# The prologue of a packed-attention and SwiGLU kernel: two moves in its written order

## The chip, the cores and the metric

The kernel runs on one core of one Trainium2 chip. The metric is the device time of the whole program in microseconds (us). The time is a median over several runs; a change of less than about 0.2% of it can't be told from none.

Engines are named as the profile names them: PE is TensorE's matrix products (PEld its loading of the stationary operand), DVE is VectorE, ACT is ScalarE, POOL is GpSimd, SP is SyncE, which here only issues DMAs.

## The reference, cut to what matters

There are 8 batches with 8 heads each, 576 positions and head size 64. A packed attention goes first: 32 packed queries `p` attend to the 576 keys and values, and then the 576 queries `q` attend to the 32 packed results, which are both keys and values there. The result, 4608 rows of 512, goes through a SwiGLU layer of width 1536 whose weights come as 64-bit numbers.

```python
def sm_attn(qq, kk, vv):
    s = scale * np.matmul(qq, kk.transpose(0, 1, 3, 2))
    s = s - np.max(s, axis=-1, keepdims=True)
    a = np.exp(s)
    a = a / (np.sum(a, axis=-1, keepdims=True) + 1e-09)
    return np.matmul(a, vv)
p_packed = sm_attn(p, k, v)
out = sm_attn(q, p_packed, p_packed)
...
g = x @ w_gate
silu = g * (1.0 / (1.0 + np.exp(-g)))
val = x @ w_val
return (silu * val @ w_out).astype(np.float32)
```

## The kernel before, in words

**Folding.** The attention's output is a weighted mean over 32 packed rows per head. So the kernel multiplies the packed rows with the gate and value weights first (`m_mm`, one matrix `mh` per batch and pair of weight chunks), and then multiplies the second attention's weights `a2` with that. Steps are named by the attention they belong to: `s1_` for the first one (scores, maximum, exponential, turning, packing, scaling), `s2_` for the second.

**Weights.** The 64-bit numbers arrive in twelve chunks of 1 MB (`load_w`, tile `st`) and are turned into fp32 by five instructions on 128x1024 elements (`f64_convert`): two on ACT (lines 124 and 125) and three on DVE, which are a clamp (line 126), a shift with an or (line 127), and an or with an and (line 128). `step("W", k)` issues the next one of the five for chunk k. A chunk's fp32 form is complete after line 128; only then may `m_mm` read it.

**Prologue.** Batch 0 has nothing to hide behind. Its stages stand in an order written by hand, within a block where PE, DVE, ACT and SP all keep the program's order; each engine runs its instructions strictly in that order, and waits where an operand isn't there. The order around the change is: load everything; the first attention's scores, exponentials, turned copies and packing (`s1_pack`, into one PSUM bank); four steps of weight chunk 0; `s1_scale` (line 288, packed result times reciprocal sum, tile `pp`); the fifth step; `s1_flip` (line 298, `pp` turned on PE) and `s1_ppt` (line 302, copied by ACT to `ppt`); the second scores of the first half of the queries, `s2_mm(0, 0)`, read by two 32x32 block transposes on DVE, `s2_block(0, 0)` (line 438); the folded weights of chunk 0, `m_mm` and `m_high` (line 524, ACT copies to `mh`); `s2_max` (lines 452 and 453) and `s2_exp` (line 457); and the second half's `s2_mm(0, 1)` and `s2_block(0, 1)`.

**Padding.** `warm_up(n)` puts n products of the identity with itself into PE's queue, with no input from any other engine. Eighteen of them stand between the scores and the first products of the SwiGLU layer, and 25 more behind those (the word `warm25` in the program's text). The profile counts two matmul records for each fp32 product.

**After the padding.** `back(0)` (line 716) turns the first half's attention weights into `a2f`. The first products of the SwiGLU layer, `gv(0)` (line 742), read `a2f` and `mh`. From there PROGRAM lists the order for the rest of batch 0 word by word (`W2` is a step of chunk 2, `g0` is `gv(0)`, `M:1.0` a folded product). Batches 1 to 7 follow in a loop with a plan by chunk.

**Banks.** PSUM has three rings here: `acc` (4 banks), `gv` (2) and `aux` (2). In the prologue `ps()` hands out `acc` and `gv` banks in turn. The scores, folded products and packing all draw on these, and `gv(0)` takes the two `gv` banks next.

Of the kernel before, what the change touches and what calls it, by code (L numbers as in the profile page):

```python
# [59 lines left out]
def tile_pack_attention_swiglu(ctx: ExitStack, tc: tile.TileContext, qT, kT, v, vq, pT, wgv, wout, out):  # L60
# [30 lines left out]
    def pin(ins):  # L91

        return tc.keep_in_program_order(ins) if steady[0] else ins

    def ps():
        turn[0] += 1
        if wide[0] and turn[0] % 2:
            return ps_acc.tile([P, 512], F32, tag="acc", name="acc_aux")
        if wide[0]:
            return ps_gv.tile([P, 512], F32, tag="gv", name="gv_aux")  # L100
        return ps_aux.tile([P, 512], F32, tag="aux", name="aux")
# [33 lines left out]
    def convert_w(fc):  # L135
        return f64_convert(w_t[fc // 2][:, :, fc % 2, :], sts.pop(fc), NHP)
# [12 lines left out]
    def convert_wout(k):  # L149
        wos[k] = pair(F32, "wo_f")  # L150
        return f64_convert(wos[k], sts.pop(("out", k)), 2)
# [13 lines left out]
    def load_k(b):  # L165
        p_t = pool.tile([P, NHP, NP], F32, tag="p", bufs=2, name="p_t")
        (nc.sync if b else nc.scalar).dma_start(p_t, pT[b])
        k_t = io_tile(0, [P, 2, NHP, HS], F32, "k_t")
        if b == 0:
            qs[b] = io_tile(0, [P, 2, NHP, HS], F32, "q_t")  # L170
        for hf in range(2):
            nc.sync.dma_start(k_t[:, hf], kT[b, :, hf])
        kps[b] = (k_t, p_t)
# [16 lines left out]
    def by_head(outs, lhs, rhs):  # L190

        for hp in range(NHP):
            for par in range(NPAR):
                r = slice(64 * par, 64 * par + 64)
                nc.tensor.matmul(outs[par][32 * hp : 32 * hp + 32], lhs(r, hp), rhs(r, hp), start=True, stop=True)  # L195
# [90 lines left out]
    def s1_scale(b):  # L286
        pp = pool.tile([P, NPAR, D], F32, tag="pp", bufs=1, name="pp")
        nc.vector.tensor_tensor(
            pp,
            pps[b][0][:, : NPAR * D].rearrange("p (r d) -> p r d", r=NPAR),  # L290
            st1[b][2][:, 2].unsqueeze(2).broadcast_to([P, NPAR, D]),
            op=ALU.mult,
        )
        pps[b].append(pp)

    def s1_flip(b):
        pps[b].append(ps())
        nc.tensor.transpose(pps[b][2][:, :P], pps[b][1].rearrange("p r d -> p (r d)"), ident)

    def s1_ppt(b):  # L300
        ppts[b] = pool.tile([P, P], F32, tag="ppt", bufs=2, name="ppt")
        nc.scalar.copy(ppts[b], pps[b][2][:, :P])
# [117 lines left out]
    def s2_tiles(b):  # L420
        st2[b] = (
            pool.tile([P, 2, NPAR, HS], F32, tag="s2", bufs=1, name="s2"),
            pool.tile([P, 3, 2 * NPAR * NBK], F32, tag="r2", bufs=1, name="r2"),
        )
# [3 lines left out]
    def s2_mm(b, c, bank=ps):  # L428
        two[b, c] = [bank(), bank()]
        q_t, ppt = qs[b], ppts[b]  # L430
        by_head(
            [x[:, :HS] for x in two[b, c]], lambda r, hp: ppt[r, 32 * hp : 32 * hp + 32],
            lambda r, hp: q_t[r, c, hp],
        )

    def s2_block(b, c):
        for par in range(NPAR):
            pin(nc.vector.transpose(st2[b][0][:, c, par], two[b, c][par][:, :HS]))

    def s2_view(b, cs):  # L440
        s2, r2 = st2[b]
        n = NPAR * NBK
        rows = slice(cs.start * n, cs.stop * n)
        return (
            s2[:, cs].rearrange("p c r (k n) -> p (c r k) n", n=NP),
            [r2[:, i, rows] for i in range(3)],
            [P, (cs.stop - cs.start) * n, NP],
        )

    def s2_max(b, cs):  # L450
        x, (m, _, _), shape = s2_view(b, cs)
        pin(nc.vector.tensor_reduce(m, x, axis=AX.X, op=ALU.max))
        pin(nc.vector.tensor_tensor(x, x, m.unsqueeze(2).broadcast_to(shape), op=ALU.subtract))  # L453

    def s2_exp(b, cs):
        x = st2[b][0][:, cs].rearrange("p c r n -> p (c r n)")
        pin(nc.scalar.activation(x, x, AF.Exp, scale=SCALE))  # L457
# [10 lines left out]
    def s2_scale(b, cs):  # L468
        x, (_, _, r), shape = s2_view(b, cs)
        pin(nc.vector.tensor_tensor(x, x, r.unsqueeze(2).broadcast_to(shape), op=ALU.mult))  # L470
# [31 lines left out]
    def m_mm(b, k, fcs, plain=False):  # L502


        if (b, k) not in ms:
            dt = F32 if plain else F32R
            ms[b, k] = tuple(
                pool.tile([P, NPAR, 2, 2 * P], dt, tag=t, bufs=2, name=t) for t in ("mh", "ml")[: 1 if plain else 2]
            )
        ppt, w = ppts[b], w_t[k]  # L510
        n = (fcs.stop - fcs.start) * 2 * P
        pss = m_ps[b, k, fcs.start] = [ps(), ps()]
        by_head(
            [x[:, :n] for x in pss], lambda r, hp: ppt[r, 32 * hp : 32 * hp + 32],
            lambda r, hp: w[r, hp, fcs].rearrange("p f n -> p (f n)"),
        )

    def m_high(b, k, fcs):
        m = ms[b, k]
        n = (fcs.stop - fcs.start) * 2 * P  # L520
        for par, x in enumerate(m_ps[b, k, fcs.start]):
            at = (slice(None), par, fcs)
            src = x[:, :n].rearrange("p (f n) -> p f n", n=2 * P)
            nc.scalar.copy(m[0][at], src)  # L524
            if len(m) > 1:
                lows.append((m[1][at], src, m[0][at].bitcast(F32)))
# [114 lines left out]
    with tc.manual_schedule(engines={mybir.EngineType.PE}):  # L641
# [19 lines left out]
        with tc.manual_schedule(  # L661
# [23 lines left out]
            def step(kind, k):  # L685

                if (kind, k) not in conv:
                    conv[kind, k] = convert_w(k) if kind == "W" else convert_wout(k)
                next(conv[kind, k], None)

            for _ in range(4):
                step("W", 0)
            s1_scale(0)
            step("W", 0)
            s1_flip(0)
            s1_ppt(0)
            s2_tiles(0)
            c0, c1 = (slice(c, c + 1) for c in range(2))
            s2_mm(0, 0)
            s2_block(0, 0)  # L700
            m_mm(0, 0, c0, True)
            m_high(0, 0, c0)
            s2_max(0, c0)
            s2_exp(0, c0)
            s2_mm(0, 1)
            s2_block(0, 1)
            load_k(1)
            load_wout(0)
            warm_up(18)
# [4 lines left out]
            def back(c):  # L714
                for par in range(NPAR):
                    nc.vector.transpose(a2f[:, par, c * HS : (c + 1) * HS], st2[0][0][:, c, par])

            s2_sums(0, c0)
            s2_scale(0, c0)
            back(0)  # L720
            wide[0] = False

            rows, accs = begin(0)
# [188 lines left out]
```

## Time and profile before

| | |
|---|---|
| median of 3 runs | 749.33 us (749.03 to 750.16) |
| profiled execution | 749.33 us, its span 747.5 us |
| mean granted PE clock | 0.998 |
| busy: PE, DVE, ACT | 736.2, 455.4, 367.9 us |

Span is the time from the first to the last instruction; 1.8 us lie outside it. Busy PE doesn't mean useful PE: the padding counts too. [...] All times in the rows are us from the start of the span.

### The profile page before, as it was taken

What the parts mean: (1) busy time and instruction counts of PE and PEld (TensorE: products, weight loads), DVE (VectorE), ACT (ScalarE), POOL (GpSimd) and SP (SyncE); (2) the same over time, 40 slices, a digit from 0 to 9 for tenths busy, and PEclk for the clock granted to TensorE, in tenths of its full rate; (3) what the DMA queues carried; (4) which work ended last, traced back from release to release, by engine and by line L of the source; (5) the groups of instructions that cost most, each with busy time, mean ns of one, the idle gap of its engine ahead of it and who ended that gap; (6) DMA issues with size and microseconds to landing.
All of it is one profiled execution on the core that took longest, in us unless ns stands there. A gap on an engine that the chain in (4) does not pass through costs nothing.

```text
span 747.5 us, 15126 instructions
## 1 busy us (share of the span) xinstructions
PE 736.2 (98%) x6280; PEld 594.8 (80%) x6280; DVE 455.4 (61%) x1004; ACT 367.9 (49%) x662; POOL 2.0 (0%) x13
## 2 busy tenths in 40 slices
PE   7999999999999999999999999999999999999998
PEld 4756666888788887887888888888888888888886
DVE  5988878665756557645765556655575555744334
ACT  3777745754516445563544535464452644533331
POOL 0000000000000000000000000000000000000000
PEclk9999999999999999999999999999999999999999
DMA  9686583202112021302112022100201000010001
GB/s 354 251 313 249 182 323 114 72 3 72 64 71 69 2 72 65 124 4 72 64 57 83 3 72 64 58 3 1 72 2 71 3 1 2 1 57 1 1 1 71
DMA packets 20004, 59.15 MB, mean 79 GB/s; under 512 B 5984, under 2 KB 7008, under 8 KB 17376
## 3 DMA queue, kind: packets, MB, share of 16 engines
q1 hardware_dynamic: 19792, 58.12, 21.5%
q8 instruction: 49, 0.80, 0.5%
q14 instruction: 19, 0.16, 0.1%
q10 hardware_dynamic: 144, 0.07, 0.0%
HBM read 48.69 MB, written 9.49 MB: 78 GB/s over the span
## 4 chain that ended last, share of the span: by engine, by line
PE 90%; DVE 4%; ACT 2%; issue 1%; DVEq 0%; ACTq 0%
PE gv L558 34%; PE acc L577 29%; PE aux L195 7%; PE gv L742 6%; PE acc L768 6%; PE aux L577 4%; PE aux L410 1%; ACT L457 1%; PE gv_aux L195 1%; PE acc L646 1%; DVE hf L569 1%; PE warm_ps L646 1%; DVE hl L539 1%; DVE s L453 1%; ACT hh L105 1%
## 5 line engine op out<-in xcount | busy, mean ns | idle before, releaser
L565 ACT ACTIVATE sg<-gv 128x256 f32<-128x256 f32 (+1 forms) x168 | 68.9, 410 | 166.0 <-PE gv L558 134.7
L558 PE MATMUL gv<-a2h,ml 128*128 128x256 f32 (+1 forms) x672 | 147.2, 300 | 2.3 <-DVE t L572 1.8
L569 DVE TENSOR_TENSOR hf<-gv,sg 128x256 f32<-128x256 f32 x168 | 70.7, 421 | 121.2 <-PE gv L558 99.1
L558 PE MATMUL gv<-a2h,mh 128*128 128x256 f32 (+1 forms) x672 | 144.2, 296 | 0.0
L558 PE MATMUL gv<-a2l,mh 128*128 128x256 f32 (+1 forms) x672 | 144.0, 296 | 0.0
L577 PE MATMUL acc<-wo_h,hl 128*128 128x512 f32 x336 | 136.2, 405 | 0.0
L577 PE MATMUL acc<-wo_l,hh 128*128 128x512 f32 x336 | 132.2, 393 | 0.0
L577 PE MATMUL acc<-wo_h,hh 128*128 128x512 f32 x336 | 131.9, 393 | 0.0
L558 PEld LDWEIGHTS gv<-a2h,ml 128*128 128x128 f32 x672 | 115.1, 189 | 19.3 <-PE gv L558 4.6
L105 ACT CAST hh<-hf 128x256 fp32r<-128x256 f32 x168 | 67.9, 404 | 102.5 <-DVE hf L569 102.4
L539 DVE TENSOR_TENSOR hl<-hf,hh 128x256 fp32r<-128x256 f32 x168 | 70.5, 419 | 78.4 <-ACT hh L105 78.4
L558 PEld LDWEIGHTS gv<-a2h,mh 128*128 128x128 f32 x672 | 108.4, 189 | 0.0
L558 PEld LDWEIGHTS gv<-a2l,mh 128*128 128x128 f32 x672 | 108.1, 189 | 0.0
L577 PEld LDWEIGHTS acc<-wo_h,hl 128*128 128x128 f32 x336 | 63.2, 188 | 34.1 <-issue 26.2
L577 PEld LDWEIGHTS acc<-wo_h,hh 128*128 128x128 f32 x336 | 63.1, 188 | 14.5
L577 PEld LDWEIGHTS acc<-wo_l,hh 128*128 128x128 f32 x336 | 63.2, 188 | 7.9
L498 DVE TENSOR_TENSOR ml<-aux,mh 128x512 fp32r<-128x512 f32 x92 | 59.0, 681 | 4.7 <-ACT mh L524 3.6
L195 PE MATMUL aux<-w,ppt 64*32 64x512 f32 (+1 forms) x784 | 52.4, 588 | 0.5 <-ACT mh L524 0.5
L524 ACT CAST mh<-aux 128x512 fp32r<-128x512 f32 x92 | 49.2, 586 | 4.9 <-PE aux L195 1.9
L565 ACT ACT_TABLE_LOAD x30 | 38.5, 1283 | 16.2 <-PE gv L558 16.1
L768 PE MATMUL acc<-wo_f,h 128*128 128x512 f32 x96 | 44.2, 594 | 0.0
L768 PEld LDWEIGHTS acc<-wo_f,h 128*128 128x128 f32 x96 | 17.3, 189 | 17.2 <-issue 16.5
(149 smaller groups left out, 755.5 us busy)
## 6 DMA issues: line engine op xcount, KB each, us to landing
st<-in_wgv SPq DMA_DIRECT2D x12, 1024.0 KB, 6.4
k_t<-in_kT SPq DMA_DIRECT2D x16, 576.0 KB, 4.8
q_t<-in_qT SPq DMA_DIRECT2D x16, 576.0 KB, 4.9
out<-ot SPq DMA_DIRECT2D x36, 256.0 KB, 2.1
v_t<-in_vq SPq DMA_DIRECT2D x6, 1280.0 KB, 5.5
st<-in_wout SPq DMA_DIRECT2D x6, 1024.0 KB, 5.5
v_t<-in_v SPq DMA_DIRECT2D x2, 1024.0 KB, 8.5
p_t<-in_pT SPq DMA_DIRECT2D x7, 64.0 KB, 2.1
```

The lines of the kernel that those rows point to most:

```text
L105: e.copy(dst, src)
L195: nc.tensor.matmul(outs[par][32 * hp : 32 * hp + 32], lhs(r, hp), rhs(r, hp), start=True, stop=True)
L498: pin(nc.vector.tensor_tensor(*lows.pop(0), op=ALU.subtract))
L524: nc.scalar.copy(m[0][at], src)
L539: low = lo.tensor_tensor(hl, src, hh.bitcast(F32), op=ALU.subtract)
L558: nc.tensor.matmul(pg[:, :n], m_[:, g, f, s * P : (s + 1) * P], a_[:, g, off : off + n], start=(i == 0), stop=(i == 5),)
L565: nc.scalar.activation(sg[:, :n], pgs[0][:, :n], AF.Silu)
L569: nc.vector.tensor_tensor(hf, pgs[1][:, o : o + 256], sg[:, o : o + 256], op=ALU.mult)
L577: nc.tensor.matmul(acc[:, :], h_[:, c : c + P], w_[fc // 2][:, fc % 2], start=(fc == 0 and i == 0), stop=(fc == NFC - 1 and i == 2),)
L646: nc.tensor.matmul(at[:, :P], ident, ident, start=True, stop=True)
L742: nc.tensor.matmul(held[i][s][:, :n], m_[:, g, f, s * P : (s + 1) * P], a_[:, g, off : off + n], start=(j == 0), stop=(j == len(todo) - 1),)
L768: nc.tensor.matmul(accs[2 * is_b + c], half(i)[:, c * P : c * P + P], wos[fc // 2][:, fc % 2], start=(fc == 0), stop=(fc == NFC - 1),)
```

## The change

It changes the written order of the prologue, and no instruction. `s1_scale` now stands ahead of the fourth step of chunk 0 (line 127), instead of behind it. The fifth step (line 128) moves behind the first half's scores, their block transposes, their maximum and their exponential. The second half's scores `s2_mm(0, 1)` go ahead of the folded product `m_mm`, and their block transposes `s2_block(0, 1)` go behind `back(0)`. The padding and the loads stay where they were in the text, behind all of these but `s2_block(0, 1)`.

```diff
-            for _ in range(4):
+            for _ in range(3):
                 step("W", 0)
             s1_scale(0)
-            step("W", 0)
             s1_flip(0)
             s1_ppt(0)
+            step("W", 0)
             s2_tiles(0)
             c0, c1 = (slice(c, c + 1) for c in range(2))
             s2_mm(0, 0)
             s2_block(0, 0)
+            s2_max(0, c0)
+            s2_exp(0, c0)
+            step("W", 0)
+            s2_mm(0, 1)
             m_mm(0, 0, c0, True)
             m_high(0, 0, c0)
-            s2_max(0, c0)
-            s2_exp(0, c0)
-            s2_mm(0, 1)
-            s2_block(0, 1)
             load_k(1)
             load_wout(0)
             warm_up(18)
...
             s2_scale(0, c0)
             back(0)
+            s2_block(0, 1)
             wide[0] = False
```

On DVE, from the clamp of chunk 0 (`w_81` is that chunk, `s_229` and `s_228` are the second scores, before and after the change):

```order
 L126 TENSOR_SCALAR w_81<-w_81 128x4x256
+L288 TENSOR_TENSOR pp<-gv_aux,rs_118 128x128
 L127 SCALAR_TENSOR_TENSOR w_81<-w_81,st 128x4x256
-L288 TENSOR_TENSOR pp<-gv_aux,rs_118 128x128
+L438 STREAM_TRANSPOSE s_228<-gv_aux 128x288
+L438 STREAM_TRANSPOSE s_228<-acc_aux 128x288
+L452 TENSOR_REDUCE r_229<-s_228 128x18
+L453 TENSOR_TENSOR s_228<-s_228,r_229 128x576
 L128 SCALAR_TENSOR_TENSOR w_81<-st,w_81 128x4x256
-L438 STREAM_TRANSPOSE s_229<-gv_aux 128x288
-L438 STREAM_TRANSPOSE s_229<-acc_aux 128x288
-L452 TENSOR_REDUCE r_230<-s_229 128x18
```

The scaling goes one instruction up. The last bit operation of chunk 0 (line 128) goes from ahead of the four instructions on the first half's scores to behind them.

On PE before, the last of the eight products of the first scores, the first and last of the eight folded products, and what follows up to `gv(0)` (the banks are numbered to tell the two sets of scores apart, 231/232 and 259/260):

```order
L195 MATMUL acc_aux_232<-q_t_95,ppt_227 32x288
L195 MATMUL gv_aux_244<-w0_81,ppt_227 32x256
L195 MATMUL acc_aux_245<-w0_81,ppt_227 32x256
L195 MATMUL gv_aux_259<-q_t_95,ppt_227 32x288
L195 MATMUL acc_aux_260<-q_t_95,ppt_227 32x288
L646 MATMUL warm_ps_89<-ident_72 128x128 x18
L742 MATMUL gv_317<-a2f_298,mh_243 128x256 x2
```

And on PE after the change, the same pieces (the two sets of scores are in banks 230/231 and 246/247):

```order
L195 MATMUL acc_aux_231<-q_t_95,ppt_225 32x288
L195 MATMUL gv_aux_246<-q_t_95,ppt_225 32x288
L195 MATMUL acc_aux_247<-q_t_95,ppt_225 32x288
L195 MATMUL gv_aux_257<-w0_81,ppt_225 32x256
L195 MATMUL acc_aux_258<-w0_81,ppt_225 32x256
L646 MATMUL warm_ps_89<-ident_72 128x128 x18
L743 MATMUL gv_317<-a2f_296,mh_256 128x256 x2
```

The folded products now stand between both sets of scores and the padding; before, the second set stood there. On ACT the exponential (line 457) goes ahead of the two copies to `mh`; SP's order is the same.

## Rows read from the trace of the kernel before

**Rows 1.** Page, parts 1 and 4: busy time by engine; shares of the chain.

```profile
PE 736.2 (98%) x6280; PEld 594.8 (80%) x6280; DVE 455.4 (61%) x1004; ACT 367.9 (49%) x662; POOL 2.0 (0%) x13
PE 90%; DVE 4%; ACT 2%; issue 1%; DVEq 0%; ACTq 0%
```

**Rows 2.** Waits of PE from 24 us to the end: total, times, longest.

```profile
PE gv L558 <- DVE t L572: 1.8, 7, 0.4
PE aux L195 <- ACT mh L524: 0.5, 1, 0.5
PE gv L742 <- ACT mh L524: 0.5, 1, 0.5
```

**Rows 3.** Chain of waits, 18.1 to 36 us: start, us, what.

```profile
18.14 5.29 PE warm_ps L646 x36
23.43 1.73 PE gv L742 x8
25.16 5.58 PE acc L646 x50
30.75 0.70 PE aux L195 x16
```

**Rows 4.** Timeline of DVE: start, us, engine, line, operation, [idle before].

```profile
13.41 1.23 DVE L127 SCALAR_TENSOR_TENSOR w<-w,st 128x1024 int32<-128x1024 int32 x1
14.56 0.28 DVE L288 TENSOR_TENSOR pp<-gv_aux,rs 128x128 f32<-128x128 f32 x1
14.76 1.22 DVE L128 SCALAR_TENSOR_TENSOR w<-st,w 128x1024 int32<-128x1024 int32 x1
16.39 0.48 DVE L438 STREAM_TRANSPOSE s<-gv_aux 128x288 f32<-128x288 f32 x1 [0.41 <-PE acc_aux L195]
...
18.73 0.48 DVE L438 STREAM_TRANSPOSE s<-gv_aux 128x288 f32<-128x288 f32 x1
...
19.62 0.75 DVE L464 TENSOR_REDUCE r<-s 128x18 f32<-128x576 f32 x1
...
21.72 0.84 DVE L716 STREAM_TRANSPOSE a2f<-s 128x288 f32<-128x288 f32 x2
22.48 0.65 DVE L126 TENSOR_SCALAR w<-w 128x1024 f32<-128x1024 f32 x1
...
27.89 2.35 DVE L128 SCALAR_TENSOR_TENSOR w<-st,w 128x1024 int32<-128x1024 int32 x2
```

**Rows 5.** Timeline of PE and PEld, 11 to 18 us, same columns.

```profile
11.89 1.81 PE L271 MATMUL gv_aux<-v_t,a 128*32 128x64 f32 x80 [0.47 <-DMA v_t<-in_v]
...
15.58 0.43 PE L195 MATMUL gv_aux<-q_t,ppt 64*32 64x288 f32 x1 [0.36 <-ACT ppt L302]
...
15.90 0.40 PE L195 MATMUL acc_aux<-q_t,ppt 64*32 64x288 f32 x1
...
16.09 0.14 PEld L195 LDWEIGHTS gv_aux<-w,ppt 64*32 64x32 f32 x2 [0.33 <-issue]
...
16.41 0.38 PE L195 MATMUL acc_aux<-w,ppt 64*32 64x256 f32 x1
...
16.93 0.69 PE L195 MATMUL gv_aux<-q_t,ppt 64*32 64x288 f32 x1
```

**Rows 6.** Timeline of ACT, same columns.

```profile
15.26 0.27 ACT L302 COPY ppt<-acc_aux 128x128 f32<-128x128 f32 x1 [2.40 <-PE acc_aux L298]
...
18.91 0.68 ACT L457 ACTIVATE s<-s 128x576 f32<-128x576 f32 x1 [1.40 <-DVE s L453]
```

**Rows 7.** Stretches: length, busy us by engine, PEclk, DMA share, GB/s.

```profile
16.97:18.14 1.17, 1.17 (x17) 0.26 (x17) 1.10 (x3) 0.54 (x2) 0.00 (x0) 0.50 1.02 413
18.14:20.36 2.22, 2.22 (x11) 2.22 (x11) 2.17 (x4) 1.45 (x2) 0.00 (x0) 0.50 0.89 273
20.36:23.43 3.07, 3.07 (x29) 3.07 (x28) 2.93 (x8) 3.07 (x5) 0.00 (x0) 1.00 1.01 398
```

**Rows 8.** Timeline of SP's DMA issues, same columns.

```profile
19.18 0.38 SPq L144 DMA_DIRECT2D st<-in_wout  x1
```

## Prediction

> **What bounds the kernel now.** I read the page's busy times first, then PE's waits, then the chain through the prologue, and last the timelines of DVE, ACT and PE around the edit. PE is busy for 98% of the span and carries 90% of the chain [rows 1]. From 24 us to the end it waits 2.8 us in all (1.8, 0.5 and 0.5) [rows 2], seven times on DVE's read of a bank and twice on ACT's emptying one, all of which PE itself has just filled. So whatever PE is late by at 24 us, it is late by at the end. The question is when PE reaches the first products of the SwiGLU layer.
>
> In the chain these start at 23.43, directly behind the 36 records of padding, which run from 18.14 for 5.29 us without a gap; behind them come 1.73 us of products, 5.58 us of the second padding, and the next folded product at 30.75 [rows 3]. The reader should see what does not stand there: DVE. It had `a2f` ready at 21.72 + 0.84 = 22.56 [rows 4], and PE took it only at 23.43. The padding is a fixed amount of work in PE's order, so the date that counts is when the padding may start, which is when the last instruction ahead of it is done.
>
> **The change part by part.** *The scaling goes ahead of line 127.* The packing ends at 11.89 + 1.81 = 13.70 [rows 5], while DVE was in line 127 from 13.41 and came to the scaling at 14.56 [rows 4]. Now DVE waits at its head and scales at about 13.75 (I add 0.05 for the hand-over), 0.81 earlier. What hangs on it goes along: flip, copy to `ppt`, scores, and the first block transpose, which came 16.39 - 14.56 = 1.83 us behind the scaling and now comes at 15.58. Line 127 starts 0.20 behind the scaling (the step from 14.56 to 14.76), at 13.95, and ends at 15.18; DVE then idles 0.40, where it idled 0.41 before [rows 4]. The new 0.44 in front of the scaling is thus lost to DVE and nothing of it is regained by shorter work.
>
> *Line 128 goes behind the maximum.* Two block transposes, the maximum and the subtraction take 18.73 - 16.39 = 2.34 us of DVE [rows 4]. So line 128 starts at 15.58 + 2.34 = 17.92 and ends at 19.14, where it ended at 14.76 + 1.22 = 15.98. That is 3.16 us later, and the folded product needs it. Before, PE went on to the folded product at 16.09, right behind the scores [rows 5]; now it can't before 19.25 (the same 0.11 behind line 128).
>
> *The second scores go ahead of the folded product.* They were 16.93 to 18.14 [rows 5, 7]; now they run right behind the first set, at about 15.3 to 16.1. Their `gv` bank is the packing's, which the scaling has emptied by 14.03. They cost PE nothing where they now are, since it waits afterwards in any case: from 16.1 to 19.25, 3.15 us. Before, PE worked through nearly all of that time.
>
> *`s2_block(0, 1)` goes behind `back(0)`.* DVE reaches the sums (line 464) at 17.92 + 1.14 = 19.06 instead of 19.62 (the exponential, at 18.91 before, moves to about 18.1 and ends by 18.8 [rows 6]). So `a2f` is ready 0.56 earlier, at 22.0, and the bank of the second scores is free at 22.4. DVE's clamp of the next chunk comes at 22.8 instead of 22.48 [rows 4]. Neither is on the path if the padding ends later than 22.4.
>
> *The clock.* PE's granted clock is 0.50 from 16.97 to 20.36 and 1.00 behind that [rows 7]. Ahead of the fall PE had next to nothing to do between the packing's end at 13.70 and the scores at 15.58 [rows 5]; in the slow stretch it worked without a pause, and then the clock rose. Rates at both levels: a set of scores took 15.58 to 15.90 + 0.40 = 16.3 at 1.00 and 1.21 at 0.50 [rows 5, 7]; the padding at 1.00 takes 5.58 / 50 = 0.112 a record [rows 3], 4.0 us for 36. Counted from its own place, 2.22 us at half rate are worth 1.11, plus 3.07 at full rate, 4.18 [rows 7]; I use 4.15. The folded product took 16.09 to 16.79 = 0.70 at full rate [rows 5], and by the ratio of the scores about 1.2 at half rate.
>
> The trace does not show how long the slow stretch gets with a gap in it. From below: it doesn't occur, the folded product ends at 19.95 and the padding at 24.1. With the clock back at 20.36 as before, the product ends at 20.4 and the padding at 24.55. From above: the whole padding runs at half rate, 8.3 us from 20.45, to 28.75. I take the stretch as ending later by the time that PE now idles in it, 20.36 + 3.15 = 23.5, because the row nearest to this case is the one where the clock rose after unbroken work. Then the padding runs 20.45 to 23.5 at half rate (worth 1.53) and 2.62 more at full rate, to 26.1.
>
> [...]
>
> *What comes behind.* `mh` is ready by about 21.2 and `a2f` with its bank by 22.4, so the end of the padding still decides. `gv(0)` starts at 26.1 instead of 23.43: 2.7 us late. The second padding and `M:1.0` follow at 33.4. The last bit operations of the next two chunks ended at 27.89 + 2.35 = 30.24 [rows 4]; DVE is some 0.3 to 0.7 us later there, ACT about 1 us (its copies to `mh` wait for the folded product, with the next chunk's two operations behind them in its order), still ahead of 33.4. These are the instructions behind the new waits, and none gets onto the path. On SP, `load_k(1)` waits for the second scores to leave `q_t` and can only go earlier; the load of the output weights behind it was issued at 19.18 [rows 8] and needs the tile that line 128 leaves at 19.14, so it goes at about the same time; I price the DMAs at nothing.
>
> The sum: -0 (earlier scores, hidden by the wait), + 2.7 (the padding starts at 20.45 instead of 18.14, which is 3.16 for the folded product's later start, less 0.85 for what stands between its start and the padding's, 1.2 now and 18.14 - 16.09 = 2.05 before; and it takes 5.65 instead of 5.29), - 0 to 1 (the two waits on ACT later [rows 2], which I keep, since they are for copies of PE's own products). The profiled execution took 749.33, which is also the median of the runs: 749.33 + 2.7 = 752.0.
>
> **The rivals.**
>
> *A shorter slow stretch.* The clock rises where it did, or never falls: padding ends at 24.55 or 24.1, +1.1 or +0.7, 750.4 or 750.0. For it: the gap falls into the slow stretch itself, where idling is free. Against: the work that ended the stretch is what the change takes out.
>
> *The padding at half rate all through.* +5.3, 754.6. For it: nothing on record has shown a rise after a gap of 3 us. Against: in the trace unbroken work brought the clock up well within the padding's length.
>
> *Given back later.* PE's waits behind 24 us are 2.8 in all [rows 2]; if DVE and ACT, which don't get later by as much, used the time to be ahead, most of the loss is returned and the time is 749.3 to 749.8. Against: the waits are on results of PE's own products some hundred ns before.
>
> *Faster: the first SwiGLU products wait for `a2f` and not for the padding.* Then the earlier sums decide: `gv(0)` at 22.4 instead of 23.43, -1.0, 748.3. It decides only if the padding is over by 22.4, so started by 18.25 and the folded product by 17.55 at full rate. That needs line 128 to end 1.7 us before the 19.14 worked out. For it: all of DVE's dates up to `a2f` do move ahead. Against: DVE starts line 128 no earlier than 17.92.
>
> **How the numbers follow.** Forecast (752.0, own range 751.0 to 753.2): 0.68. Shorter slow stretch: 0.16. All at half rate: 0.05. Given back: 0.07. Faster: 0.04. The range 750.0 to 753.4 leaves out the returned and the faster case and the half-rate one, 0.16, and takes in the shorter stretch. The bound of 0.2% is 1.5 us, so no change reaches from 747.8 to 750.8. Slower: 0.68 + 0.05 and a fifth of the shorter stretch, 0.76. Same: the rest of that and the returned case, 0.20. Faster: 0.04.
>
> **What would show it.** Right: in PE's timeline a gap of about 3 us behind two sets of scores, ended by DVE's line 128; the folded products at about 19.2; granted clock 0.50 beyond 20.4; padding without a gap directly ahead of `gv(0)` at 25 to 27; DVE's `a2f` ready near 22, some 4 us unused; and the same length from `gv(0)` to the end. Wrong: `gv(0)` released by DVE; folded products before 18; or PE's distance from `gv(0)` to the end shorter by over 1 us.

## The result and the profile after

The changed kernel takes 752.86 us (median of 5, 752.46 to 754.38) against 749.33 us (748.65 to 750.36) before; the ratio is 1.0044, with a 95% interval of 1.0031 to 1.0058. That is 3.5 us slower, inside the range and on the side that was forecast, and 0.9 above the forecast of 752.0. The profiled execution is the median one, with a span of 751.1 us.

The timeline of DVE after the change (start, length, engine, line, operation, idle time before it) answers to [rows 4]:

```profile
14.29 0.29 DVE L288 TENSOR_TENSOR pp<-gv_aux,rs 128x128 f32<-128x128 f32 x1 [0.91 <-PE gv_aux L271]
14.50 1.22 DVE L127 SCALAR_TENSOR_TENSOR w<-w,st 128x1024 int32<-128x1024 int32 x1
16.13 0.48 DVE L438 STREAM_TRANSPOSE s<-gv_aux 128x288 f32<-128x288 f32 x1 [0.42 <-PE acc_aux L195]
...
18.47 1.22 DVE L128 SCALAR_TENSOR_TENSOR w<-st,w 128x1024 int32<-128x1024 int32 x1
19.61 0.75 DVE L464 TENSOR_REDUCE r<-s 128x18 f32<-128x576 f32 x1
...
21.70 0.84 DVE L716 STREAM_TRANSPOSE a2f<-s 128x288 f32<-128x288 f32 x2
22.46 0.44 DVE L438 STREAM_TRANSPOSE s<-gv_aux 128x288 f32<-128x288 f32 x1
```

DVE waits for the packing at the head of its queue (0.91), idles 0.42 again until the scores, and finishes line 128 at 19.69, where it was 15.98. The attention weights `a2f` are there at 22.54, as before. PE's timeline after, answering to [rows 5]: the last product of the second scores, the first of the folded products, and both paddings around `gv(0)`.

```profile
16.12 0.40 PE L195 MATMUL acc_aux<-q_t,ppt 64*32 64x288 f32 x1
19.84 0.60 PE L195 MATMUL gv_aux<-w,ppt 64*32 64x256 f32 x1 [3.31 <-DVE w L128]
...
20.88 6.06 PE L646 MATMUL warm_ps<-ident 128*128 128x128 f32 x36
26.77 1.89 PE L743 MATMUL gv<-a2f,mh 128*128 128x256 f32 x8
28.50 5.74 PE L646 MATMUL acc<-ident 128*128 128x128 f32 x50
```

PE stands still for 3.31 us, released by line 128. The chain of waits after (start, length, what) answers to [rows 3]:

```profile
18.56 1.15 DVE w L128
...
20.95 5.99 PE warm_ps L646 x36
26.93 1.73 PE gv L743 x8
28.66 5.58 PE acc L646 x50
34.24 0.70 PE aux L195 x16
```

Line 128 is now in the chain, and behind it every piece keeps its length but the padding, 5.99 instead of 5.29. `gv(0)` starts at 26.93 instead of 23.43, 3.50 later; from there to the end of the span it is 751.1 - 26.93 = 724.2 us, and before it was 747.5 - 23.43 = 724.1. Nothing was given back. The stretches (length, busy us of PE, PEld, DVE, ACT and POOL, granted clock of PE, DMA share, GB/s), answering to [rows 7]:

```profile
17.00:18.00 1.00, 0.00 (x0) 0.00 (x0) 0.96 (x2) 0.00 (x0) 0.00 (x0) 0.90 0.97 393
18.00:19.00 1.00, 0.00 (x0) 0.00 (x0) 1.00 (x2) 0.35 (x1) 0.00 (x0) 0.50 0.91 376
...
20.95:24.31 3.36, 3.36 (x16) 3.36 (x17) 3.33 (x7) 3.29 (x5) 0.00 (x0) 0.50 1.04 413
24.31:26.93 2.62, 2.62 (x23) 2.62 (x23) 2.58 (x4) 2.62 (x4) 0.00 (x0) 0.94 0.23 88
```

The clock reads 1.00 up to 17.75 and falls at about 17.8. It reads 0.50 up to 24.60 and 1.00 from 24.80, and so rises at about 24.6 (0.94 over 2.62 us is 0.31 us at 0.50 and the rest at 1.00). It is at 0.50 for 6.8 us instead of the 3.4 of [rows 7]. Half and full rate stand here for a clock of 0.50 and of 1.00: at 0.50, from 20.95 to 24.31, 16 records of padding took 3.36 us, 0.21 each, against 5.58 / 50 = 0.112 at 1.00 [rows 3].

### The profile page after: what moved, and what is told of

Same layout as the page of the kernel before. It is cut to its first block, busy times and chain, and to the rows that moved or that the text cites. A ratio compares the mean times of both kernels' runs of the same rounds, so it can differ in the third digit from the quotient of the medians.

```text
span 751.1 us, 15127 instructions
## 1 busy us (share of the span) xinstructions
PE 737.4 (98%) x6280; PEld 595.8 (79%) x6280; DVE 456.1 (61%) x1004; ACT 368.6 (49%) x662; POOL 2.0 (0%) x13
## 4 chain that ended last, share of the span: by engine, by line
PE 92%; DVE 4%; ACT 2%; issue 1%; POOL 0%; DVEq 0%; ACTq 0%; POOLq 0%
PE gv L558 34%; PE acc L577 29%; PE aux L195 7%; PE gv L743 6%; PE acc L769 6%; PE aux L577 4%; PE aux L410 1%; PE warm_ps L646 1%; ACT L457 1%; PE gv_aux L195 1%; PE acc L646 1%; DVE s L453 1%; DVE hf L569 1%; DVE hl L539 1%; DVE r L452 1%
```

## The experiments

Two theories stood against each other. The first is the prediction's: line 128's date holds the folded product, PE idles, and both the late start and the longer stretch at the half rate push the padding and all that follows. The rivals put the loss on other moves of the change, or deny the clock a part in it. Each ratio below is to the kernel before as timed beside that run. Its median there was 749.58 us for the four kernels with line 128 early, line 128 late, 8 and 10, and 7 and 18, and 749.16 us for the other four; small differences between two kernels are therefore taken from the ratios.

**Line 128 early again, the rest as changed.**

```diff
             s1_ppt(0)
             step("W", 0)
+            step("W", 0)
             s2_tiles(0)
...
             s2_exp(0, c0)
-            step("W", 0)
             s2_mm(0, 1)
```

> The change with one part of it undone: chunk 0's last bit operation (line 128) again directly behind line 127, the rest as changed. Theory: line 128's date is what holds the folded product, so that product starts at about 17.0 instead of 19.84, PE hardly idles in front of it, and the padding ends near 23.3; the clock's slow stretch is then about as in the kernel before. gv(0) near 23.5, total 749.3 (748.6 to 750.0). Rival: the loss comes from the other moves (the second scores ahead, their transposes behind the first half's turning, the scaling); then the time stays near 752.9.

Measured: 749.15 us, ratio to before 0.9995 (0.9986 to 1.0003). The whole loss is gone; the other moves cost nothing that can be measured. PE's timeline of this kernel, the first of the folded products, the first padding and `gv(0)`:

```profile
17.14 0.40 PE L195 MATMUL gv_aux<-w,ppt 64*32 64x256 f32 x1 [0.90 <-DVE s L438]
...
17.73 4.29 PE L646 MATMUL warm_ps<-ident 128*128 128x128 f32 x36
22.55 1.97 PE L743 MATMUL gv<-a2f,mh 128*128 128x256 f32 x8 [0.54 <-ACT st L125]
```

The folded product came at 17.14, as expected, but what it waited for last was a bank that DVE still read (line 438); line 128 was done by then. The padding ran at full rate (the granted clock is 1.00 throughout in this execution) and ended at 22.0, so `gv(0)` came not at 23.5, as expected, but at 22.55. The wait is put down to an instruction of ACT on a weight chunk, which `gv(0)` doesn't read; I take only the date from it. DVE's timeline names the likelier one:

```profile
21.93 0.84 DVE L716 STREAM_TRANSPOSE a2f<-s 128x288 f32<-128x288 f32 x2
22.69 0.44 DVE L438 STREAM_TRANSPOSE s<-gv_aux 128x288 f32<-128x288 f32 x1
```

`gv(0)` starts 0.62 behind the start of the two transposes that write `a2f`, and ahead of the read of the second scores' bank at 22.69.

**Line 128 late, the rest as before.**

```diff
             s1_scale(0)
-            step("W", 0)
             s1_flip(0)
...
-            m_mm(0, 0, c0, True)
-            m_high(0, 0, c0)
             s2_max(0, c0)
             s2_exp(0, c0)
+            step("W", 0)
+            m_mm(0, 0, c0, True)
+            m_high(0, 0, c0)
             s2_mm(0, 1)
```

> The kernel before with one part of the change alone: line 128 and with it the folded product go behind the first half's maximum and exponential; scaling, second scores and their transposes stay where they were. Theory: the folded product starts at about 20.1, with PE idle from 16.3 on, and now the second scores stand between it and the padding too, so gv(0) comes at about 27.5 and the time is 753.4 (752.6 to 754.5). Rival (the other moves are the cause): 749.3 to 750.3.

Measured: 753.62 us, ratio 1.0053 (1.0041 to 1.0065). This part alone costs as much as the change. A little more was expected, since the second scores again stand between the folded product and the padding; the two intervals overlap, so that surcharge is not shown. Its waits of PE (who waited, for what: total us, times, longest):

```profile
PE gv_aux L195 <- DVE w L128: 3.8, 1, 3.8
```

**The scaling early, the rest as before.**

```diff
-            for _ in range(4):
+            for _ in range(3):
                 step("W", 0)
             s1_scale(0)
-            step("W", 0)
             s1_flip(0)
             s1_ppt(0)
+            step("W", 0)
+            step("W", 0)
```

> The kernel before with another part of the change alone: the packed result is scaled ahead of lines 127 and 128, which follow it directly; nothing else moves. Theory: the scores come earlier, but lines 127 and 128 each end later by what DVE waited for the packing (0.3 to 0.9 us, with the packing's date in that execution), so the folded product starts at 16.4 to 16.9 instead of 16.09, and padding and gv(0) stay within half a us: 749.6 (749.0 to 750.3). Rival (the earlier scaling is worth its 0.8 us): 748.8. Rival (it is the scaling that costs the change its time): over 751.

Measured: 749.79 us, ratio 1.0004 (0.9993 to 1.0015): no difference that can be told. The first part of the change neither costs nor gains. PE's timeline shows the folded product waiting for the later line 128, as expected, and then something that was not expected:

```profile
16.86 0.37 PE L195 MATMUL gv_aux<-w,ppt 64*32 64x256 f32 x1 [1.08 <-DVE w L128]
...
17.94 4.29 PE L646 MATMUL warm_ps<-ident 128*128 128x128 f32 x36
22.58 1.97 PE L743 MATMUL gv<-a2f,mh 128*128 128x256 f32 x8 [0.35 <-DVE a2f L717]
```

The granted clock was 1.00 throughout in this execution. All 18 padding products stand there, and `gv(0)` still waited 0.35 us for `a2f`. So at full rate the padding was over before `a2f` was ready here, and DVE decided.

**The same 18 padding products, 8 of them in the gap.**

```diff
             s2_mm(0, 1)
+            warm_up(8)
             m_mm(0, 0, c0, True)
...
-            warm_up(18)
+            warm_up(10)
```

> The change with the same 18 padding products, 8 of them ahead of the folded product and 10 behind it. Theory: the 8 fill the gap that line 128 leaves (16.5 to 19.8), the folded product starts as before that edit, the clock is back at full rate by about 20.4 since PE doesn't idle, and the 10 end at about 23.0, where a2f and its bank are just ready: gv(0) at 23.1, total 749.0 (748.3 to 749.8), no slower than the kernel before although line 128 is as late as in the change. Rival (the slow stretch has nothing to do with the gap and lasts to 24.3 again): the 10 end at 24.9, total 750.8.

Measured: 748.72 us, ratio 0.9993 (0.9983 to 1.0003), against 752.86 for the change itself. Line 128 is as late as in the change here (it ends 5.40 us behind the start of the scaling in both), and the loss is gone. PE's timeline:

```profile
15.83 2.05 PE L646 MATMUL warm_ps<-ident 128*128 128x128 f32 x16
19.21 0.37 PE L195 MATMUL gv_aux<-w,ppt 64*32 64x256 f32 x1 [1.33 <-DVE w L128]
...
19.80 2.50 PE L646 MATMUL warm_ps<-ident 128*128 128x128 f32 x20
22.14 1.89 PE L744 MATMUL gv<-a2f,mh 128*128 128x256 f32 x8
```

The 8 ended at 17.9, still 1.2 us ahead of line 128's end, and the clock never fell in this execution. So the expectation that it would fall near 17 and come back was wrong, and it came out better: `gv(0)` at about 22.3.

**7 more products in the gap, 18 behind as in the change.**

```diff
             s2_mm(0, 1)
+            warm_up(7)
             m_mm(0, 0, c0, True)
```

> The change with 7 more padding products, ahead of the folded product; all 18 stay behind it. It has more work on PE than the change. Theory: the late start stays (folded product at about 19.8), but the gap is filled, so the clock is back by about 20.4 and the 18 take 4.2 to 4.4 us instead of 5.99: gv(0) at 25.1, total 751.1 (750.6 to 751.7), that is 1.8 faster than the change with more work. Rival (the gap doesn't set the clock): 752.9 as in the change.

Measured: 750.46 us, ratio 1.0014 (1.0005 to 1.0022). More work on PE than the change, and 2.4 us less time (2.2 by the ratios). PE's timeline of the 7, the folded product and the 18 (two records for each padding product), then the stretches with the granted clock behind ACT's and POOL's columns:

```profile
16.02 1.83 PE L646 MATMUL warm_ps<-ident 128*128 128x128 f32 x14
19.41 0.37 PE L195 MATMUL gv_aux<-w,ppt 64*32 64x256 f32 x1 [1.55 <-DVE w L128]
...
20.00 4.29 PE L646 MATMUL warm_ps<-ident 128*128 128x128 f32 x36
24.12 1.89 PE L744 MATMUL gv<-a2f,mh 128*128 128x256 f32 x8
```

```profile
18.00:19.00 1.00, 0.00 (x0) 0.00 (x0) 1.00 (x2) 0.68 (x1) 0.00 (x0) 1.00 0.95 396
19.00:20.00 1.00, 0.59 (x16) 0.21 (x16) 0.96 (x3) 0.00 (x0) 0.00 (x0) 1.00 1.00 375
20.00:21.00 1.00, 1.00 (x16) 1.00 (x9) 0.93 (x3) 0.85 (x3) 0.00 (x0) 1.00 1.04 417
```

This run splits the loss. With the gap's first half filled the clock stays at 1.00, the 36 records take 4.29 instead of 6.06, and what is left, 0.14% or 1.0 us, is the late start. The other 0.30% of the change, 2.2 us, is the clock. The 1.0 us is counted against the kernel before as it comes, and most of the executions timed beside this run had a mean clock below 1.000 themselves. Against the 8 of those 29 that had 1.000 (median 749.08), the 11 of 12 here with 0.999 or 1.000 (median 750.37) are 1.3 us later.

**8 padding products instead of 18, all behind the folded product.**

```diff
-            warm_up(18)
+            warm_up(8)
```

> The change with 8 padding products instead of 18, behind the folded product as there. Theory: late start and slow clock stay, folded product 19.84 to 20.95 at half rate, the 8 end at about 22.8, gv(0) at 22.9 and itself at half rate until about 24.3, so its products end at 25.5 instead of 28.66: about 3 less than the change, 749.9 (749.2 to 750.8). Rival (gv(0) waits for DVE or ACT and the padding only fills): 752.9, as in the change.

Measured: 749.70 us, ratio 1.0006 (0.9995 to 1.0017). Ten products fewer give 3.2 us back (2.8 by the ratios), so in the changed kernel `gv(0)` waited for padding, not for DVE or ACT. The gap of 3.31 us and a slow stretch are both still there, but in this execution the stretch ran only from 19.0 to 22.5, 3.4 us, where it was 6.8 in the change. The timeline of PE and two stretches:

```profile
19.17 0.60 PE L195 MATMUL gv_aux<-w,ppt 64*32 64x256 f32 x1 [3.31 <-DVE w L128]
...
20.20 3.11 PE L646 MATMUL warm_ps<-ident 128*128 128x128 f32 x16
23.15 1.89 PE L743 MATMUL gv<-a2f,mh 128*128 128x256 f32 x8
```

```profile
19.00:20.00 1.00, 0.83 (x16) 0.26 (x16) 0.93 (x4) 0.00 (x0) 0.00 (x0) 0.52 1.02 379
...
22.00:23.00 1.00, 1.00 (x9) 1.00 (x8) 1.00 (x3) 1.00 (x2) 0.00 (x0) 0.77 1.02 407
```

**The kernel before with 14 padding products instead of 18.**

```diff
-            warm_up(18)
+            warm_up(14)
```

> The kernel before with 14 padding products ahead of gv(0) instead of 18, no other edit. Theory (in the kernel before, too, the padding and not DVE decides when gv(0) starts): gv(0) at about 22.65, as soon as a2f is there, 0.8 earlier: 748.7 (748.2 to 749.2) against 749.5. Rival (DVE decides, or PE gives it back in later waits): no change, 749.5.

Measured: 748.87 us against 749.16, ratio 0.9990 (0.9981 to 0.9999). In its profile `gv(0)` now waits:

```profile
18.10 3.39 PE L646 MATMUL warm_ps<-ident 128*128 128x128 f32 x28
22.46 1.97 PE L742 MATMUL gv<-a2f,mh 128*128 128x256 f32 x8 [0.97 <-DVE a2f L716]
```

So with 14 products DVE decides. This execution does not show that 4 products more would have changed that: the clock was back at 1.00 when its padding began, and 36 records at that rate, 4.29 us as in the kernel with the scaling early, would by this estimate have ended at 22.39, just ahead of 22.46. That the padding decided in the profiled execution of the kernel before is read from [rows 3] and [rows 4], where a stretch at the half rate had made it 5.29 us long. The time follows by 0.1% only (0.7 us by the ratio), at the edge of what can be told, which fits a padding that decides in some executions and not in others.

**And 22 in the second padding instead of 25.**

```diff
-    W2 g0 ... W2 warm25 W1
+    W2 g0 ... W2 warm22 W1
...
-            warm_up(18)
+            warm_up(14)
```

> The same with 22 products in the second padding instead of 25 as well. Theory: gv(0) as with 14, the next folded product (M:1.0) at about 29.25, just behind the bit operations it needs (29.1 in the profile before), M:0.1 just behind 30.24: 1.4 less than before, 748.1 (747.6 to 748.6). Rival (those bit operations hold PE already): as with 14 alone, 748.7.

Measured: 749.25 us, ratio 0.9995 (0.9985 to 1.0006): the expected 1.4 us did not come. In its profiled execution the granted clock was 0.50 from 14 to 18 us, and the packing, which began at 11.80, was slow too (2.83 us, where it took 1.81 in [rows 5]):

```profile
11.80 2.83 PE L271 MATMUL gv_aux<-v_t,a 128*32 128x64 f32 x80 [0.80 <-DMA v_t<-in_v]
...
23.13 1.97 PE L742 MATMUL gv<-a2f,mh 128*128 128x256 f32 x8 [1.00 <-DVE a2f L716]
24.93 5.07 PE L646 MATMUL acc<-ident 128*128 128x128 f32 x44
29.95 0.67 PE L195 MATMUL aux<-w,ppt 64*32 64x256 f32 x16
```

The scaling, and all of DVE behind it, was late by that, and `gv(0)` comes when DVE lets it, 0.67 later than with 14 alone. `M:1.0` (29.95) stands directly behind the shorter second padding, without a wait, and came there at the same time as with 14 alone (29.93). One profile does not show whether that holds for the twelve timed runs, which spread from 748.16 to 750.16; why this kernel gains less than the one with 14 and 25 stays open.

The version that keeps the change and splits its padding 8 and 10 has the lowest median seen, 748.72; it beats the change clearly, and the kernel before by less than can be told.

## Why the prediction was right

**Which wait ends last.** The step that decided everything was to see that 18 products without operands stand ahead of `gv(0)`, so that the date of the last instruction ahead of them counts, not `a2f`. For the changed kernel the run with 8 products shows it: it gives some 3 us back with nothing else changed. The run with line 128 early shows that this instruction sets when the padding starts.

For the kernel before, the step holds only for an execution like the profiled one. There `gv(0)` came 0.87 us behind `a2f`, at the end of a padding that ran partly at the half rate. With the scaling early and with line 128 early, both at 1.00 throughout, the same padding was over before `a2f`. In the executions of the kernel before at full rate, `a2f` has therefore probably decided; none of them was profiled. The forecast does not fail by it, since the padding of the changed kernel ends over 4 us behind `a2f`.

**DVE's dates.** Worked out: scaling 13.75, line 128 from 17.92 to 19.14, folded product 19.25. Measured: 14.29, 18.47 to 19.69, 19.84. All are late by the same 0.54 to 0.59, and that comes in with the packing: it began at 12.36 here and at 11.89 before. Ahead of it the order did not change, and in the other profiles it began between 11.67 and 12.21, so this is one execution's spread and not the change. The hand-over to the scaling, 0.05, was my estimate from no row; here it was 14.29 - (12.36 + 1.86) = 0.07. The distances between the dates were right within 0.05; PE's gap was 3.31 where 3.15 was worked out. By the same token `a2f` did not come 0.56 earlier in this execution; in the kernel with padding 8 and 10, whose scaling was at 13.66, its two transposes start at 21.06 instead of 21.72, as the step has it.

One point was wrong without a price: the second scores' bank was named as something `gv(0)` must wait for. With line 128 early `gv(0)` starts before that bank is read, so its first products use another one.

**The clock.** It was taken that the slow stretch ends as much later as PE idles in it, at 23.5; it began at 17.8 instead of 16.97 and ended at 24.6, and the padding took 5.99 instead of 5.65. This is the term that was too small. In time it is 0.34, beside the 0.54 from the packing; the folded product took 1.11 where 1.2 was taken. Together that is the 0.8 us between 26.1 and 26.93.

That the stretch grows by the idle time is not borne out as a rule. With 8 products the gap is again 3.31 us, and the stretch lasted 3.4 us in the profiled execution. By the mean clock, six of that kernel's twelve executions were like this one (0.997), while none of the changed kernel's five was above 0.995. Nor does any run show that it was the unbroken work of [rows 7] that ended the stretch there; the row shows only that the clock rose at 20.36, behind 3.39 us of it. So the size that this step gave fits the changed kernel, and its reason does not carry over; that it came so close is in part luck.

The rival with the clock back early priced the late start alone at 0.7 to 1.1; the run with 7 products more measured 1.0 for it (1.3 among executions at full rate), so that rival's price was about right for a kernel whose gap is partly filled. The rival with the whole padding at half rate did not occur: the clock rose within the padding, at about 24.6. Nothing was returned later, as [rows 2] had it: PE's waits behind 24 us are now 1.3, 0.5 and 0.5.

```profile
PE gv L558 <- DVE t L572: 1.3, 6, 0.2
PE aux L195 <- ACT mh L524: 0.5, 1, 0.5
PE gv L743 <- ACT mh L524: 0.5, 1, 0.5
```

The gain in the first of them, 0.5, is about as large in most of the other profiles (1.3 or 1.4 in six of them), with faster and slower ones alike, so it is not the change's.

## What to carry to other kernels

Padding in an engine's queue has a length of its own: look for what must end before it can start, and check with the trace whether the engine reaches the real work behind it because of the operands or because of the padding. When an instruction is moved back on one engine, ask which engine then stands still, and whether there is filler behind the wait that could stand ahead of it: the same 18 products, split around the wait, brought back the whole loss (748.72 us instead of 752.86). And take the clock of several executions before a trace of one is read: here the padding came last in a profile of the kernel before that has a stretch at the half rate, and `a2f` came last in the profiles of two variants without one. Earlier results are worth nothing on a path that doesn't end with them.

## What the runs showed of the hardware

The granted clock of the same kernel differs between executions. Of 35 timed executions of the kernel before, 18 had a mean clock of 1.000, with most of their times from 748.4 to 749.4, and the two with 0.993 took 750.6 and 751.2. In another 29 it was 1.000 in only 8. All five of the changed kernel had 0.991 to 0.995. With 7 products in the gap 11 of 12 had 0.999 or 1.000, and the one with 0.993 took 752.75, 2.3 above that kernel's median. So the profile before, with its 3.4 us at the half rate, was one of several forms of the same kernel. With a gap of PE of 3.3 us none of 17 executions (the change's 5, and 12 with 8 products) had a mean clock above 0.997. The 7 products took 1.83 us at the start of that gap and left 1.55 us of it in the profile; that 11 of 12 stood so high with that was not expected.

What starts a slow stretch stays open. A gap of 3.3 us did not stand ahead of every one: in the profile before, PE never stood still for more than 1.20 us from 1.35 us up to the fall at 16.9. Nor is the place the same: of the two kernels with 14 products, whose order up to there is the same, the one with 25 behind them had a mean clock of 0.59 from 14 to 17, which puts the fall at about 14.5 (an estimate: 0.41 / 0.50 of 3 us is 2.5 us at 0.50), and the one with 22 had 0.50 in all of that stretch, so that it fell before 14. With the scaling early, whose profile has a gap of 1.08 us, 10 of 12 executions had a mean clock of 0.993 to 0.998.
